# Batch 0 of a sparse attention with a dense layer behind it: halo keys on their own partitions, block keys scored apart, value rows cast in place, and two q turns moved into the output stage

## The chip, the cores and the metric

The kernel runs on one core of a Trainium2 chip. The metric is the device time of one execution in microseconds (us), over several executions (a run counts as slow when it is over 1.5% above the fastest of its kernel). A profile is one execution recorded by the hardware. In its lines PE is TensorE's matmuls, PEld its weight loads, DVE is VectorE, ACT is ScalarE, POOL is GpSimd, SP is SyncE.

## The reference, cut to what matters

```
q, k, v: (4 batches, 8 heads, 768 rows, 64) float32
k_sum = k in blocks of 32 rows: max over the block      # 24 block keys
v_sum = v in blocks of 32 rows: mean over the block     # 24 block values
scores_l = scale * q k^T, kept only where |row - col| < 16
scores_s = scale * q k_sum^T + log(32)
a = softmax over both together
x = a [v ; v_sum]                                       # (3072, 512) over all heads
h = x w_in (512 x 2048);  out = (h * sigmoid(1.702 h)) w_out (2048 x 512)
```

So each row looks at its neighbours within 15 rows and at 24 block rows.

## The kernel before

The work goes in eight halves: u = 0 to 7 are the two halves of batches 0 to 3. Each half has a dense input stage (`ph`, 64 matmuls of 384 columns), an activation, and a dense output stage (`po`, 48 of 512). The attention of half u+1 is slipped between the `po` matmuls of half u. Batch 0's first half has nothing before it: that is the prologue.

Tokens go in tiles of 64. In `kx` each tile has 128 key columns: 64 own keys, 24 block keys and 32 halo keys (neighbours; 8 columns stay empty), so one matmul scores all of them. The values `vw` need the rows in the same order on the partitions, so neighbours' rows have to cross partitions. DMAs inside SBUF do that:

```python
def before_even(w5, j0, j1):
    sp.dma_start(out=w5[96:112, j0:j1, 0], in_=w5[112:128, j0 - 1:j1 - 1, 1])
...                                   # after_even, before_odd, after_odd alike
def q_now(p):                         # first half of batch 0: two heads on 128 partitions
    return qz[p].rearrange("p t h c -> p (t h c)")[:, 0:HALF]
def s_turn(p):                        # scores of batch 0's first half, 64-row tiles
    big = st["S", p] = psb.tile([128, 1024], F32, name="ps_s", tag="big")
    for i in range(TH):
        for h in range(2):
            r = slice(h * 64, h * 64 + 64)
            pe.matmul(out=big[:, h * 512 + i * QT:h * 512 + i * QT + QT],
                      lhsT=kx[p][0][r, i, :], rhs=q_now(p)[r, i * QT:i * QT + QT],
                      start=True, stop=True)
```

Every other half keeps q padded with zeros (`qz`, both heads side by side), so that one matmul of 128 columns scores two heads. `psb`, tag "big", has two PSUM buffers that rotate between k turns, q turns, scores and values. The joint of the prologue, and the preparation of a batch in the second half of the one before:

```python
load_q(0, 0, 1) ... load_q(0, 3, 1)     # late q: second half of batch 0
s_exp(2); s_turn(3); v_zero(pool); s_exp(3)
v_cast(4, 0, act); v_cast(5, 0, act, 1); v_cast(5, 0, pool, 0)
load_w_in(0); load_w_in(1); load_w_in(2); load_w_in(3)
...
todo = {1: [lambda: tk(0, s)], 2: [lambda: tk(1, s)], 4: [lambda: tk(2, s)],
        6: [lambda: tk(3, s)], 8: [lambda: vsum(s, (0, 1, 2))],
        9: [lambda: vsum(s, (3, 4, 5)), lambda: vrows(s)],
        10: [lambda: tq(0)], 11: [lambda: tq(1)],
        13: [lambda: tq(2)], 14: [lambda: tq(3)]}
for nt in range(NT):                    # 16 groups of four ph matmuls
    ff_in(u, nt)
    for f in todo.get(nt, ()):
        f()
```

The softmax here doesn't subtract the row's maximum and nothing guards it: scores larger than these inputs give would overflow.

## Time and profile before

| | before |
|---|---|
| median of 3 runs (lowest to highest) | 241.51 us (241.22 to 242.05) |
| span of the profiled run | 239.8 us |
| first `ph` matmul (end of the prologue) | 26.63 us |
| input, output stage of half 0 | 13.96, 13.89 us |
| input, output stage of half 1 (prepares batch 1) | 16.16, 14.32 us |
| input, output stage of halves 3 and 5 (batches 2, 3) | 14.5, 13.89 us each |
| the same without a batch to prepare (halves 2, 4, 6) | 10.52, 13.9 us |

The stages are read on TensorE's timeline, from the first `ph` (or `po`) to the first of the next stage. The prediction below shows the busy row, the waits, TensorE's timeline and the chain.

VectorE's timeline in the prologue (start, duration, engine, line, operation, output and inputs, their shapes):

```profile
14.95 0.54 DVE L27 CAST qz<-ps_q 128x384 bf16<-128x384 f32 x1
15.42 0.41 DVE L27 CAST vw<-vf 64x512 bf16<-64x512 f32 x1
15.75 0.54 DVE L27 TENSOR_TENSOR a_sb<-a_sb,mk 128x768 bf16<-128x768 bf16 x1
18.84 1.53 DVE L27 TENSOR_TENSOR a_sb<-a_sb,mk 128x768 bf16<-128x768 bf16 x2 [2.55 <-ACT a_sb L27]
```

SyncE's share is not the halo copies, though: 22.9 of its 25.0 us lie between 41.3 and 65.2, where it issues batch 1's loads, the last of which TensorE then waits for (the q wait). On SyncE's timeline:

```profile
41.96 8.77 SPq L27 DMA_DIRECT2D kf<-in_k_dram  x8
...
57.69 8.09 SPq L27 DMA_DIRECT2D qf<-in_q_dram  x8
```

VectorE stands idle for 2.55 us in the middle of the prologue. Its casts take 0.41 and its mask multiplies 0.54.

### The profile page before, as it was taken

To read this page: it belongs to the slowest core of one execution; us is meant where nothing else is said; L and a number is where in the kernel's file an instruction comes from. 1 tells how busy PE (TensorE), PEld (TensorE's weight loads), DVE (VectorE), ACT (ScalarE), POOL (GpSimd) and SP (SyncE) were. 2 spreads that over 40 slices of the span, in tenths; PEclk is the share of its full clock that TensorE was granted. 3 is DMA by queue.
4 is the path that set the end of the run, shared out by engine and by line. 5 is a ranking of instruction groups with operands and counts; after the bars stand their busy time and mean duration, and the time that the engine had idled before them with its cause. 6 is when DMAs were issued, how large, how long until landed. Compare 5 with 4: busy or idle time off the path is not lost.

```text
span 239.8 us, 4567 instructions
## 1 busy us (share of the span) xinstructions
PE 226.7 (95%) x1743; PEld 132.7 (55%) x1743; DVE 128.5 (54%) x328; ACT 132.6 (55%) x225; POOL 69.9 (29%) x142
## 2 busy tenths in 40 slices
PE   7786979999989999999999999999999999999993
PEld 2533646556555555556665556556665565556541
DVE  5774945586964810486975800596957700770000
ACT  3856446455446467754565477545574478457510
POOL 6579960048640005773000013971000000000000
PEclk9999999999999999999999999999999999999999
DMA  6996999999993169995051199993051110111012
GB/s 194 286 192 103 238 231 206 222 218 218 202 260 98 45 156 219 201 220 173 0 113 46 44 195 202 231 223 119 14 102 45 44 46 0 44 46 44 0 44 89
DMA packets 76534, 32.21 MB, mean 134 GB/s; under 512 B 63856, under 2 KB 73440, under 8 KB 76512
## 3 DMA queue, kind: packets, MB, share of 16 engines
q1 hardware_dynamic: 72288, 27.73, 53.4%
q0 software_dynamic: 4224, 4.19, 10.7%
q8 instruction: 13, 0.21, 0.4%
q14 instruction: 9, 0.07, 0.1%
HBM read 27.26 MB, written 6.29 MB: 140 GB/s over the span
## 4 chain that ended last, share of the span: by engine, by line
PE 71%; SPq 10%; DMA 10%; DVE 3%; POOL 2%; issue 1%; ACT 0%; POOLq 0%; ACTq 0%
PE po L27 30%; PE ph L27 28%; SPq L27 10%; DMA w_in_sb<-in_moe_w_in_dram 7%; PE ps_av L27 4%; PE ps_s L27 3%; PE ps_t L27 2%; PE ps_x L27 2%; DMA kf<-in_k_dram 2%; DVE ks L27 1%; DMA qf<-in_q_dram 1%; PE ps_vs L27 1%; DVE kx L27 1%; POOL w_in_sb L27 1%; POOL vw L27 1%
## 5 line engine op out<-in xcount | busy, mean ns | idle before, releaser
L27 PE MATMUL po<-w_out_sb,gT 128*128 128x512 bf16 x384 | 95.6, 379 | 0.0
L27 PE MATMUL ph<-xT,w_in_sb 128*128 128x384 bf16 x512 | 91.6, 326 | 1.7 <-DMA w_in_sb<-in_moe_w_in_dram 1.6
L27 ACT ACTIVATE gT<-ph 128x384 bf16<-128x384 f32 x128 | 62.9, 491 | 40.2 <-PE ph L27 40.2
L27 PEld LDWEIGHTS <-w_in_sb 128*128 128x128 bf16 x512 | 48.7, 98 | 32.4 <-DMA w_in_sb<-in_moe_w_in_dram 2.4
L27 PEld LDWEIGHTS <-gT 128*128 128x128 bf16 x384 | 34.6, 98 | 28.0
L27 DVE TENSOR_TENSOR a_sb<-a_sb,mk 128x768 bf16<-128x768 bf16 x32 | 19.3, 609 | 55.8 <-ACT a_sb L27 55.0
L27 ACT ACTIVATE a_sb<-ps_s 128x768 bf16<-128x768 f32 x32 | 25.2, 809 | 23.0 <-PE ps_s L27 22.9
L27 POOL CAST kb<-kf 128x768 bf16<-128x768 f32 (+1 forms) x15 | 11.5, 765 | 78.8 <-DMA kf<-in_k_dram 78.8
L27 DVE TENSOR_TENSOR x_sb<-ps_av,rc 64x384 bf16<-64x384 f32 (+1 forms) x60 | 33.2, 554 | 1.4
L27 ACT ACTIVATE osb<-po 128x512 f32<-128x512 f32 x24 | 14.2, 593 | 31.3 <-issue 15.6
L27 POOL CAST vw<-vf 128x512 bf16<-128x512 f32 (+2 forms) x45 | 27.8, 659 | 3.2 <-DMA vf<-in_v_dram 3.0
L27 ACT ACT_TABLE_LOAD x16 | 20.5, 1283 | 1.1 <-PEq L792 0.8
L27 PEld LDWEIGHTS <-a_sb 128*128 128x128 bf16 (+1 forms) x264 | 13.8, 102 | 10.2 <-issue 2.7
L27 PE MATMUL ps_av<-vw,a_sb 128*128 128x130 bf16 (+1 forms) x216 | 15.8, 214 | 2.0 <-DMA vw<-vw 1.8
L27 PEld LDWEIGHTS <-kx 128*128 128x128 bf16 (+1 forms) x216 | 12.4, 97 | 6.6 <-issue 0.8
L27 PE MATMUL ps_s<-qz,kx 128*128 128x128 bf16 (+1 forms) x216 | 15.3, 213 | 0.1
L27 DVE COPY qz<-ps_t 64x768 bf16<-64x768 bf16 x24 | 13.3, 555 | 2.9 <-PE ps_t L27 2.5
L27 POOL CAST qb<-qf 128x768 bf16<-128x768 f32 (+1 forms) x14 | 11.4, 812 | 8.8 <-DMA qf<-in_q_dram 8.5
L27 DVE COPY xT<-ps_x 128x384 bf16<-128x384 bf16 x30 | 10.7, 358 | 3.7 <-PE ps_x L27 2.9
L27 PEld LDWEIGHTS <-x_sb 128*128 128x128 bf16 x96 | 7.7, 97 | 8.0 <-issue 1.8
L27 DVE RECIPROCAL rc<-ps_av 128x12 f32<-128x12 f32 (+1 forms) x32 | 7.2, 226 | 8.5 <-PE ps_av L27 8.2
L27 DVE TENSOR_REDUCE ks<-ps_t 128x24 bf16<-128x768 bf16 x12 | 11.4, 946 | 0.0
(61 smaller groups left out, 141.5 us busy)
## 6 DMA issues: line engine op xcount, KB each, us to landing
kf<-in_k_dram SPq DMA_DIRECT2D x32, 192.0 KB, 3.6
qf<-in_q_dram SPq DMA_DIRECT2D x32, 192.0 KB, 4.6
vf<-in_v_dram SPq DMA_DIRECT2D x24, 256.0 KB, 5.2
out_dram<-osb SPq DMA_DIRECT2D x24, 256.0 KB, 2.3
w_in_sb<-in_moe_w_in_dram POOLq DMA_DIRECT2D x4, 512.0 KB, 11.1
w_out_sb<-in_moe_w_out_dram POOLq DMA_DIRECT2D x4, 512.0 KB, 18.8
vw<-vs SPq DMA_DIRECT2D x6, 148.5 KB
vw<-vw SPq DMA_DIRECT2D x6, 99.0 KB, 2.9
```

Source lines behind the costliest of these rows:

```text
L27: r = f(*a, **kw)
```

## The change

In batch 0, `kx` keeps the 64 own keys and a 32-row neighbour strip on each side, each on the partitions that those rows have anyway; the block keys are scored by a matmul of their own. The value rows can then be cast from the staged float32 straight to where they belong, without a DMA. Both halves of batch 0 use this form. The intent is to take the copies through SyncE out of the prologue, and the weights forward.

```diff
+    def k_blocks(p, eng):
+        eng.tensor_copy(out=ksz[0:64, p, 0:nb], in_=st["m", p][0:64])
+        eng.tensor_copy(out=ksz[64:128, p, 32:32 + nb], in_=st["m", p][64:128])
+    def b_turn(p, half=0):                      # block scores, apart
...
+        r = slice(p % 2 * 64, p % 2 * 64 + 64)
+        pe.matmul(out=st["Bs", p // 2][r, 0:HALF], lhsT=ksz[:, p, :], rhs=q_now(p, half),
+                  start=True, stop=True)
+    def v_side(j, par, eng):                    # neighbours' value rows, in place
+        r, c = (slice(0, 32), j + 1) if par else (slice(96, 128), j - 1)
+        copy(eng, vw[0][r, 2 * j + par, :, 0:D], raw["v", c // 2][r, :, c % 2, :])
... the prologue's order
-    before_even(w50, 1, JH)                     # and ten more halo copies by DMA
-    load_q(0, 0, 1)                             # to load_q(0, 3, 1)
+    v_side(2, 1, dve)
     s_exp(2)
...
     s_exp(3)
+    v_cast(4, 0, dve)
...
     load_w_in(0)
+    v_sum(3)
+    v_idle(1)
+    v_cast(5, 0, dve, 0)
+    av_near(0)
...
     load_w_in(1)
+    s_mask(3, pool)
...
+    sp.dma_start(out=hold, in_=xT[0][0:16, 0:16])
+    for p in range(NP):
+        load_q(0, p, 1)
     load_w_in(2)
     load_w_in(3)
... preparation of the next batch
-                    10: [lambda: tq(0)], 11: [lambda: tq(1)],
-                    13: [lambda: tq(2)], 14: [lambda: tq(3)]}
+                    12: [lambda: tq(0)], 14: [lambda: tq(1)]}
+            later = {1: lambda: tq(2), 3: lambda: tq(3)}      # between the po groups
...
+            if u == 1 and nt == 7:
+                for p in range(NP):
+                    clear_qz(dve, p, 0)
+                    clear_qz(dve, p, 1)
```

The small DMA into `hold` reads `xT`, so that SyncE's queue stands until `xT` is there; the late q is issued behind it. One more thing changes: of the filler matmuls in the prologue (`warmth`, `v_idle`: their results are not used, they only keep TensorE busy), 17 behind the first eight become 5.

## The prediction

> **What bounds the kernel now.** I read the busy share of every engine first, then TensorE's waits, then the chain that ended last over the first 45 us, then TensorE's timeline around the places where it waits.
>
> ```profile
> PE 226.7 (95%) x1743; PEld 132.7 (55%) x1743; DVE 128.5 (54%) x328; ACT 132.6 (55%) x225; POOL 69.9 (29%) x142
> ```
>
> TensorE (PE) is busy for 226.7 of 239.8 us, and no other engine passes 55%. So time can only be won in TensorE's own work, or where it stands idle. The view of its waits says how little idle there is:
>
> ```profile
> PE ps_av L27 <- DMA vw<-vw: 1.8, 1, 1.8
> PE ph L27 <- DMA w_in_sb<-in_moe_w_in_dram: 1.6, 1, 1.6
> PE ps_t L27 <- POOL qb L27: 1.1, 1, 1.1
> ```
>
> One wait each: for the halo rows of the values, which a DMA copies from partition to partition inside SBUF; for the first weights; and, at 65.7 us, for batch 1's q. Everything else is the order of work. The kernel is a prologue (attention of batch 0, first half, until 26.6 us) and then eight pairs of a dense input stage (`ph`) and output stage (`po`), the latter with the next half's attention slipped between. The timeline of TensorE shows the joint:
>
> ```profile
> 20.67 0.38 PE L27 MATMUL ps_vt<-vw,E 128*128 128x512 bf16 x1
> ...
> 23.00 0.51 PE L27 MATMUL ps_av<-vw,a_sb 128*64 128x65 bf16 x21 [1.77 <-DMA vw<-vw]
> ...
> 26.63 5.65 PE L27 MATMUL ph<-xT,w_in_sb 128*128 128x384 bf16 x32
> 33.83 0.82 PE L27 MATMUL ph<-xT,w_in_sb 128*128 128x384 bf16 x4 [1.56 <-DMA w_in_sb<-in_moe_w_in_dram]
> ```
>
> The first 32 `ph` matmuls are half of the stage (two of four weight chunks); then the third chunk is not there. The chain confirms that what ends last here is not attention but the weights, behind GpSimd's (POOL) queue:
>
> ```profile
> 17.37 1.71 POOL vw L27 x2
> 19.07 2.28 POOL w_in_sb L27 x3
> 21.36 15.92 DMA w_in_sb<-in_moe_w_in_dram
> 37.28 0.05 issue
> 37.33 0.82 PE ph L27 x4
> ```
>
> The fourth chunk is issued at 21.4 and lands at 37.28, and TensorE starts on it 0.05 us later: the whole input stage stands on this transfer. Its packet records say why it takes so long: a chunk of 512 KB takes 2.54 us when alone (the w_out chunks end at 38.30, 40.84, 43.38) but 4.0 us while the late q loads and the halo copies run too (w_in chunks end at 24.36, 28.37, 32.37).
>
> After 40.6 us it is nearly solid. Measured on the timeline, the output stage of half 0 takes 13.89 (40.59 to 54.48); batch 1's preparation stage 16.16 (54.48 to 70.64), against 14.5 for the same stage of batch 2 (109.50 to 124.00): the 1.7 us are the wait for q (1.07) and VectorE (DVE), which is busy without a gap from 56.4 to 66.6.
>
> **What the Trainium skill says.** "DMA: Bandwidth & Descriptors", Anatomy of one DMA, gives a fixed cost of about 2 us, mostly the receipt after the last byte. The trace agrees in size: the last packet of the third chunk ends at 32.37 and TensorE goes on at 33.83, 1.46 us later. The same page, Issuing engines are not separate DMA queues, says that DMAs of all issuers share the same 16 engines and interleave: that is the 2.54 against 4.0 us per chunk. "ScalarE: Activation LUTs", What ACT_TABLE_LOAD costs, has 1283 ns per load plus a drain; the trace has 1283 ns as the mean of 16 loads. It matters below, because it stands ahead of the first exp of each output stage. No page tells how the two rotating PSUM buffers below are handed on; that is read from the kernel.
>
> **The change, part by part.**
>
> *1. Prologue: the wait and GpSimd's detour go.* Value rows and their neighbours are now cast from the staged tile straight to their partitions, so the 1.77 us wait for the copies goes. I chained the new order of instructions with durations of the old profile. The values arrive as before: by the packet records the six transfers end 1.25 apart, the fourth at 14.52 (it landed 1.3 later, at 15.83), the fifth at 15.79, and the sixth, into which the halo copies came, at 17.57. Without them I put it at 17.05 and its landing at 18.3 (the old run cast it from 18.69). VectorE: the last k_max ends at about 13.1 (four reductions of 0.94, the side copies 0.27 to 0.33), then casts and masks at 0.41 to 0.54 bring it to 17.7. ScalarE (ACT): fourth exp until 16.9, block exp 17.3, then the last values from 18.3 to 18.7. So the last v_sum pair runs at about 18.7 to 19.1 instead of 20.45 to 20.9: 1.7 us earlier. From there to the first `ph` the old order took 26.63 - 20.45 = 6.2, of which 1.8 is the wait; the new one has the same chain (four small copies, four normalisations of 0.54 on VectorE, transposes, xT copies) of some 4.2. Start about 22.9: 3.7 earlier.
>
> *2. Weights.* GpSimd reaches the first w_in issue after its casts at about 15.8 (k and q casts until 11.4; side copies 1.0; the casts 0.64 to 0.72 each, with one wait for k_max at 13.1), where it was 19.03. The packets started 1.6 after the issue (20.61), so 17.4 now. The halo copies (0.4 MB) are gone and the late q loads start only after xT. Alone, five chunks (four w_in and the first w_out) take 12.7; the old run took 38.30 - 20.61 = 17.7, a penalty of 5.0 for 1.2 MB of strangers; two thirds of those remain, penalty 3.3. The first w_out chunk then ends at 33.4 and lands at 34.9. The w_in chunks land in time, so the stage takes 64 x 0.163 + 4 q turns x 0.29, with 0.3 at the start: 11.9 instead of 13.96. 22.9 + 11.9 = 34.8, and w_out allows 34.9: the first output stage starts at 34.9 instead of 40.59, **5.7 earlier**.
>
> *3. Output stage of half 0 grows.* Half 1 of batch 0 now also scores apart. Per pair of heads: scores 0.28 (12 small matmuls, prologue's pitch) against 0.34; block scores 384 columns, 0.16, new; near values 0.34 against 0.34; block values 3 x 130 columns, 0.17, new. That is +0.27, times four **+1.1**. ScalarE gets two more exps of 0.49, VectorE fewer instructions; neither is last there. Net at 54.48: -4.6.
>
> *4. Batch 1's preparation.* Turning q2 and q3 in the output stage takes the q wait (1.07) off. But qz of batch 0 is no longer zero-padded, so 16 memsets of 0.218 (3.5 us) now stand on VectorE between the fourth k and the block sums, in the stretch where it has no gap. With T the start of the stage, VectorE's k work ends T+10.4 as before, memsets T+14, block sums T+14.6, q0 copies T+15.8. TensorE is through at T+14.6 (14.5, as batch 2, plus 0.9 for VectorE's late buffers, less 0.7 for two turns moved), runs one `po` group (0.87) and meets the first scores at T+15.5: they wait 0.3 to 0.8 for q0. Then the rest of part 5. In all about **-0.4** against the old 30.5 for both stages.
>
> *5. Two q turns between the scores, batches 2 and 3.* They are taken out of the input stage (0.34 each) and put in the output stage, so work is the same. But turned q and scores share two rotating PSUM buffers: the order becomes s0, q2, s1, and s1 must wait for s0's exp, where s0 and s1 used to have a buffer each. In batch 2's stage (start F = 124.00) the exp ends at F+2.76 behind the table load; s1 would start at F+2.06+0.34 = F+2.4. Wait 0.4. Later VectorE's q copies (1.14 a pair) delay the first normalisation, and v1, which reuses v0's buffer, loses about 0.2. So **+0.6** each for batches 2 and 3, 1.2 together; batch 2 and 3 had no q wait to win back.
>
> Sum: -5.7 + 1.1 - 0.4 + 1.2 = -3.8. 241.5 - 3.8 = 237.7 us, 1.6% faster.
>
> **Rivals.** (a) *Everything early stays won, nothing is paid later*: if the buffers rotate more kindly than I read them and the memsets hide, -5.7 + 1.1 - 1.5 = -6.1, 235.4. For it: the two-buffer wait is read from code, no old view shows it. Against: VectorE has no gap at 56 to 66. (b) *The transfer is the bound anyway*: the gain of the prologue is lost to w_out or batch 1's loads. These began landing in the old run when w_out ended (47.6) and run at about 0.22 MB/us for 21 us; if GpSimd reaches w_in only at 18, all moves with it: about 240. For it: the old chain runs through this very transfer; against: the gap in DMA traffic at 18 to 20 us (share 0.16), which the earlier issue fills. (c) *VectorE becomes the bound of the prologue*: it takes over side copies and casts; if they run slower beside GpSimd (a 128x384 cast took 0.36 alone and up to 0.77 in company), the start slips by 1 to 1.5: 239.
>
> **Range and chances.** The prologue is chained by hand through five engines, +-1; the later costs +-0.8; GpSimd's issue +-0.8. Together about 1.7 either way. 2% is 236.7, one microsecond below my figure: faster by more 0.28, within 2% 0.68, slower 0.04.
>
> **What would show it.** Right: no wait for vw<-vw in the prologue; first `ph` at 22 to 23.3; first w_in issue near 15.8; no or a short wait for w_out at the first `po`, near 34.9; output stage of half 0 at 15.0; no wait for qb in batch 1, but one for qz at its first scores; batches 2 and 3 taking 0.6 longer from their preparation to the end of the output stage. Wrong: a first `ph` after 24.5, a w_in issue after 18, batch 2's stages unchanged in length, or the memsets hidden.

## More of the kernel before

The page's summary of the chain that ended last, by engine:

```profile
PE 71%; SPq 10%; DMA 10%; DVE 3%; POOL 2%; issue 1%; ACT 0%; POOLq 0%; ACTq 0%
```

## The result, and the profile after

| | before, same rounds | after |
|---|---|---|
| median (lowest to highest), 4 runs each | 241.78 us (241.22 to 242.21) | 248.2 us (248.09 to 250.15) |
| span of the profiled run | 239.8 us | 246.6 us |

The ratio is 1.0286 (95% interval 1.023 to 1.0342): the changed kernel is slower. All ratios here are the mean time of one kernel's fast runs over that of the other's of the same rounds, so not quite the ratio of the medians quoted. The predicted 237.7 us, its range, and its likeliest class (within 2%) are all missed.

The stages say where the time came from:

| stage | before | after | difference | predicted |
|---|---|---|---|---|
| prologue, to the first `ph` | 26.63 | 28.14 | +1.5 | -3.7 |
| half 0, input | 13.96 | 13.36 | -0.6 | -2.1 |
| half 0, output | 13.89 | 15.83 | +1.9 | +1.1 |
| half 1, both (prepares batch 1) | 30.48 | 32.60 | +2.1 | -0.4 |
| halves 3 and 5, both | 28.4 each | 29.3 each | +0.9 each | +0.6 each |

That is 6.7 of the 6.8 us between the spans: half 2 gives 0.1 back, and the rest lies behind the start of the last stages.

Three rows of the page of the changed kernel: busy time of each engine, the granted TensorE clock in 40 slices (in tenths; 9 is full), and the chain by engine:

```profile
PE 228.5 (93%) x1727; PEld 132.4 (54%) x1751; DVE 130.4 (53%) x322; ACT 134.2 (54%) x228; POOL 76.6 (31%) x170
...
PEclk9998899999999999999999999999999999999998
...
PE 70%; DVE 15%; DMA 7%; ACT 3%; issue 2%; SPq 2%; ACTq 0%; DVEq 0%
```

SyncE's share of the chain has gone from 10% to 2%, and VectorE's has risen from 3% to 15%. Most of SyncE's fall is not the copies: batch 1's loads are no longer on the path, as its q is no longer what TensorE waits for, and VectorE's work for batch 1 has taken their place. That the copies are off the path shows in the waits below. The clock row shows an 8 in slices 4 and 5, which the profiled run of the kernel before does not have; other runs of that kernel have a mean granted clock down to 0.98, so a stretch at half clock is not a mark of the changed kernel alone. The waits of TensorE (total, times, longest):

```profile
PE ps_s L27 <- DVE qz L27: 3.3, 1, 3.3
PE ps_vs L27 <- DVE vw L27: 2.1, 3, 1.5
PE ps_av L27 <- DVE vw L27: 1.6, 1, 1.6
PE ps_q L27 <- DVE qz L27: 1.4, 1, 1.4
```

Waits for the halo copies and for w_in are gone. All four that replace them name VectorE. On TensorE's timeline they lie thus:

```profile
20.14 0.48 PE L27 MATMUL ps_av<-vw,a_sb 128*64 128x65 bf16 x19 [1.61 <-DVE vw L27]
...
22.37 0.38 PE L27 MATMUL ps_vs<-vw,E 128*128 128x512 bf16 x1 [1.52 <-DVE vw L27]
...
38.90 0.49 PE L27 MATMUL ps_q<-ident,qb 128*128 128x128 bf16 x3 [1.37 <-DVE qz L27]
...
75.78 0.51 PE L27 MATMUL ps_s<-qz,kx 128*128 128x128 bf16 x6 [3.31 <-DVE qz L27]
```

The first two are in the prologue, the third in the input stage of half 0, the fourth in the output stage of half 1. What VectorE and GpSimd did before the first two:

```profile
17.70 2.38 DVE L27 CAST vw<-vf 32x512 bf16<-32x512 f32 x1
...
18.20 1.64 POOL L27 DMA_DIRECT2D w_in_sb<-in_moe_w_in_dram  x2
...
19.85 2.19 POOL L27 TENSOR_TENSOR a_sb<-a_sb,mk 128x768 bf16<-128x768 bf16 x1
20.01 0.53 DVE L27 TENSOR_TENSOR a_sb<-a_sb,mk 128x768 bf16<-128x768 bf16 x1
20.48 2.05 DVE L27 CAST vw<-vf 128x512 bf16<-128x512 f32 x2
```

A cast of 32 x 512 takes 2.38 us here; a larger one took 0.41 before. The row with two casts, 2.05 together, is 1.84 and 0.28 one by one. VectorE is not busy in these 4 us so much as held. The slow cast of 1.84 us lies beside GpSimd's mask multiply, which runs from 19.85 to 22.04, and ends 0.28 after it. The cast of 2.38 us lies mostly beside two issues of weight loads, in front of that multiply.

The third and fourth wait, on the timeline of SyncE's queue and of VectorE (that of the latter from two stretches):

```profile
28.07 2.38 SPq L27 DMA_DIRECT2D qf<-in_q_dram  x4
...
38.02 0.36 DVE L27 CAST qb<-qf 128x384 bf16<-128x384 f32 x1 [3.37 <-DMA qf<-in_q_dram]
...
69.31 4.66 DVE L27 MEMSET qz<- 64x192 uint32 x16
```

The late q is issued at 28.07 and its last part can be cast at 38.02. All four casts stand in VectorE's order ahead of the first copy of turned q (`qz`), so TensorE waits for it. In batch 1, sixteen memsets stand in front of the block sums and of the q copies.

### The profile page after: what moved, and what is told of

Read it like the earlier page. It is cut to its first block, busy times and chain, and to the rows that moved or that the text cites. A ratio compares the mean times of both kernels' runs of the same rounds, so it can differ in the third digit from the quotient of the medians.

```text
span 246.6 us, 4562 instructions
## 1 busy us (share of the span) xinstructions
PE 228.5 (93%) x1727; PEld 132.4 (54%) x1751; DVE 130.4 (53%) x322; ACT 134.2 (54%) x228; POOL 76.6 (31%) x170
## 4 chain that ended last, share of the span: by engine, by line
PE 70%; DVE 15%; DMA 7%; ACT 3%; issue 2%; SPq 2%; ACTq 0%; DVEq 0%
PE po L27 27%; PE ph L27 26%; PE ps_av L27 5%; DVE qz L27 4%; PE ps_s L27 3%; DMA qf<-in_q_dram 3%; DVE x_sb L27 3%; DVE kx L27 3%; PE ps_t L27 2%; PE ps_x L27 2%; DMA vf<-in_v_dram 2%; DMA kf<-in_k_dram 2%; DVE vw L27 2%; ACT a_sb L27 2%; SPq L27 2%
## 5 line engine op out<-in xcount | busy, mean ns | idle before, releaser
L27 PE MATMUL po<-w_out_sb,gT 128*128 128x512 bf16 x361 | 92.1, 379 | 1.1
L27 PE MATMUL ph<-xT,w_in_sb 128*128 128x384 bf16 x512 | 90.2, 326 | 0.0
L27 PEld LDWEIGHTS <-w_in_sb 128*128 128x128 bf16 x512 | 49.2, 98 | 30.9 <-issue 1.5
L27 DVE TENSOR_TENSOR x_sb<-ps_av,rc 64x384 bf16<-64x384 f32 (+1 forms) x56 | 30.9, 555 | 1.6 <-PE ps_av L27 0.2
L27 POOL CAST vw<-vf 128x512 bf16<-128x512 f32 (+2 forms) x49 | 31.2, 674 | 1.2 <-DMA vf<-in_v_dram 0.6
L27 ACT ACT_TABLE_LOAD x16 | 20.5, 1283 | 1.1 <-PEq L858 0.8
L27 PE MATMUL ps_s<-qz,kx 128*128 128x128 bf16 (+1 forms) x240 | 14.8, 208 | 4.0 <-DVE qz L27 3.3
L27 PEld LDWEIGHTS <-a_sb 128*128 128x128 bf16 (+1 forms) x240 | 12.4, 106 | 10.6 <-issue 3.9
L27 PEld LDWEIGHTS <-kx 128*128 128x128 bf16 (+1 forms) x240 | 11.3, 97 | 11.5 <-DVE qz L27 5.3
L27 POOL CAST qb<-qf 128x768 bf16<-128x768 f32 (+1 forms) x16 | 12.4, 772 | 8.0 <-DMA qf<-in_q_dram 7.2
L27 PE MATMUL ps_x<-ident,x_sb 128*128 128x128 bf16 x96 | 10.6, 219 | 0.8 <-DVE xT L27 0.6
```

Source lines behind the costliest of these rows:

```text
L27: r = f(*a, **kw)
```

## The experiments

My theory after reading the traces was that five things make the loss: VectorE's casts held in the prologue, TensorE's half clock behind that, the late q, the memsets in batch 1, and the late turns. The expectations call "port lock" the theory that VectorE's casts and GpSimd cannot use SBUF at the same time. The main rivals were that the weight issues hold the casts and not the multiply, and that the transfers bound the first input stage whatever the prologue does. Twelve kernels ran; all gave correct results. Each is compared with the kernel before in the same rounds; "the changed kernel" is the one of the section above.

### The mask multiply from GpSimd to VectorE

```diff
-    s_mask(3, pool)
+    s_mask(3, dve)
```

> The changed kernel with the fourth mask multiply back on VectorE. Theory (port lock): a VectorE copy from SBUF cannot run while GpSimd holds the port they share, whether GpSimd multiplies, casts or issues a weight load. Then the four weight issues now follow one another (0.8 us each, about 18.2 to 21.4) and hold the side cast of the values until 21.4 instead of 20.08, while the cast held by the multiply until 22.04 comes free: little is won, 0 to 0.7 us, 247.5 to 248.2. Rival (only the multiply blocks, the issues do not): the side cast takes 0.4, both PE waits of 1.6 and 1.5 shrink, and 2 to 3 us are won, about 245.5.

Measured: median 248.76 us (247.46 to 250.26), ratio 1.0267 (1.0203 to 1.033). VectorE and GpSimd in the prologue of this kernel, from their timelines:

```profile
17.89 0.82 DVE L27 CAST vw<-vf 32x512 bf16<-32x512 f32 x1
18.64 0.54 DVE L27 TENSOR_TENSOR a_sb<-a_sb,mk 128x768 bf16<-128x768 bf16 x1
19.11 1.03 DVE L27 CAST vw<-vf 128x512 bf16<-128x512 f32 x2
...
18.39 3.11 POOL L27 DMA_DIRECT2D w_in_sb<-in_moe_w_in_dram  x4
```

The same cast takes 0.82 instead of 2.38, and the next two 0.41 and 0.69 instead of 1.84 and 0.28, although GpSimd is issuing weight loads nearly all the while (for the first 0.5 us it still casts). So the issues alone do not hold a cast for 2 us: that reading falls, and the multiply is what does. An issue may still cost some 0.4, as the last and smallest cast is slower here. The first `ph` comes at 24.16 instead of 28.14. Yet no time was won: the input stage now takes 17.9 us instead of 13.36, because its q turns wait 2.7 us for `qb` and 2.6 us for `qz`, and the output stage starts 0.6 later than in the changed kernel. There are two bounds behind one another. Half 1 lost another 1.1 us (33.71), with the clock at half from 76.4 to 79.8.

### The late value casts from VectorE to ScalarE

```diff
-    v_side(2, 1, dve)          # and v_cast(4, 0, dve), v_cast(5, 0, dve, 0)
     v_cast(3, 0, act)
+    v_side(2, 1, act)
...
-    v_cast(5, 0, act, 1)
+    v_cast(4, 0, act)
+    v_cast(5, 0, act)
```

> The changed kernel with the three value casts that VectorE did late in the prologue (a side cast of 32 partitions, 128x512, 128x256) on ScalarE; the fourth mask stays on GpSimd. Theory (port lock): ScalarE is not held by GpSimd, so the casts take 0.6 each, the near products start at about 18.3 instead of 20.14, no wait for vw remains, and the first ph comes at about 24.5 to 25 instead of 28.14: about 245. Rival (VectorE and ScalarE just have too much work in the prologue, the 2.38 us were queueing): ScalarE becomes late instead, first ph after 27, within 1 us of 248.2.

Measured: 249.3 us (247.31 to 251.2, one run slow), ratio 1.0275 (1.0226 to 1.0324). First `ph` at 24.45, input stage 17.59. The multiply stayed on GpSimd and took 1.66 us instead of 2.19; the difference is as long as the one mask multiply on VectorE that lay beside it in the changed kernel (0.53). So leaving the multiply and moving the casts heals the prologue as well; it looks as if the two engines disturb each other, and the stage behind it gives everything back again (the output stage starts at 42.04, not 41.50).

### Both together

The two edits above in one kernel.

> Both edits: fourth mask on VectorE, the three casts on ScalarE. Theory (port lock): no VectorE copy from SBUF is left next to the weight issues; first ph at 23.5 to 24.5, clock stays at full speed, total about 4 us less: 244. The masks (two SBUF inputs) may still be held a little. Rival (prologue is bound by the arrival of the values or of the weights): first ph no earlier than 26, and a wait for w_in appears.

Measured: 249.75 us (247.39 to 250.5), ratio 1.0305 (1.0247 to 1.0363). First `ph` at 23.98, output stage at 40.67 instead of 41.50. In the profiled run the late q was issued at 23.72, 4.35 us earlier than in the changed kernel. VectorE's timeline, and then TensorE's:

```profile
37.19 0.36 DVE L27 CAST qb<-qf 128x384 bf16<-128x384 f32 x1 [1.78 <-DMA qf<-in_q_dram]
...
38.07 0.49 PE L27 MATMUL ps_q<-ident,qb 128*128 128x128 bf16 x3 [2.71 <-DVE qz L27]
```

The last part is cast only 0.83 us earlier than in the changed kernel. The late q shares the DMA engines with 2 MB of w_in and with w_out, and lands at about 37 to 38 whether it is issued at 23.7 or at 28.1. That is why 4.2 us of prologue are worth 0.8 us at the output stage. These 0.8 us were lost in turn: the output stage of half 1 took 21.34 us instead of 18.49, with the granted clock at half from 74.1 to 80.9.

### More filler matmuls in the two gaps

```diff
-    v_idle(1)                  # ahead of the near values
+    v_idle(8)
...
     v_recip(0)
+    v_idle(6)
```

> The changed kernel with 13 more filler matmuls in the two places where TensorE idled for 1.6 and 1.5 us. The trace granted half the clock from 23.1 to 26.5 us. Theory (the clock fell because of the two gaps, and cost time): the clock stays at 1.0 and the first ph comes 0.7 to 1.2 us earlier, about 247.2. Rival (the halved clock hid behind VectorE's chain): clock 1.0, first ph within 0.3 of 28.14, 248. If the clock falls all the same, the gaps were not its cause.

Measured: 247.81 us (245.5 to 249.1), ratio 1.0231 (1.0161 to 1.03); at 2% that is unclear, and its interval overlaps that of the changed kernel. The windows view says what the filler did. Its columns are busy time with instructions for PE, PEld, DVE, ACT and POOL, then granted clock, DMA share and GB/s. First the changed kernel, in two windows of 3.4 us:

```profile
19.70:23.10 3.40, 1.45 (x29) 0.98 (x29) 3.00 (x6) 0.00 (x0) 3.39 (x4) 1.00 1.02 155
23.10:26.50 3.40, 3.40 (x44) 2.01 (x43) 1.60 (x6) 2.03 (x4) 3.21 (x6) 0.50 1.24 205
```

Then the kernel with filler:

```profile
19.70:23.10 3.40, 2.86 (x35) 1.50 (x35) 2.90 (x6) 0.00 (x0) 3.39 (x4) 1.00 1.04 160
23.10:26.50 3.40, 3.13 (x54) 2.03 (x52) 2.67 (x8) 2.87 (x6) 3.21 (x6) 1.00 1.24 206
```

Where TensorE was busy for 1.45 of 3.40 us, the next 3.4 us ran at half clock; with 2.86 of 3.40 they did not. In the profiled run the first `ph` came at 26.87 instead of 28.14 with the casts held just as long (2.38): the half clock is worth 1.3 us there, by one execution of each kernel. In the other three runs of this kernel the mean clock was 0.99 again (where it fell is not recorded), so filler is not a sure cure.

### The memsets of qz out of batch 1's preparation

```diff
-            if u == 1 and nt == 7:
-                for p in range(NP):
-                    clear_qz(dve, p, 0)
-                    clear_qz(dve, p, 1)
...
                 else:
                     tx(p)                    # batch 0's second half
+                    clear_qz(dve, p, 1)
...
         if u == 0:
+            for p in range(NP):
+                clear_qz(dve, p, 0)
```

> The changed kernel with the 16 memsets of qz taken out of batch 1's preparation: half 0 is cleared on VectorE during the first input stage, where it is idle, half 1 behind the xT copies of the first output stage. Theory: the memsets (4.66 us in the trace) are what makes the first scores of batch 1 wait 3.3 us; the wait falls to 0 to 0.5 and the total by about 3: 245.2. Rival (VectorE's k work, which ends at 69.3, or the arrival of q sets that stage): the wait stays above 2, total within 1 us of 248.2.

Measured: 245.59 us (244.87 to 247.73), ratio 1.0166 (1.0112 to 1.0221). Half 1 takes 13.85 + 15.43 = 29.28 us instead of 32.60, and the wait of the first scores for `qz` is gone. What is left at the scores, on TensorE's timeline:

```profile
75.00 0.49 PE L27 MATMUL ps_s<-qz,kx 128*128 128x128 bf16 x6 [0.30 <-ACT a_sb L27]
```

This is the wait for a PSUM buffer behind the exp, which the prediction's part 5 spoke of. The memsets are worth 3.3 us of the stage, the largest part that any single edit gave back. The input stage of half 0 took 14.70 in this profiled run (13.36 in the changed kernel), so not all of it shows in the time.

### The two late turns back in the input stage

```diff
-                    12: [lambda: tq(0)], 14: [lambda: tq(1)]}
-            later = {1: lambda: tq(2), 3: lambda: tq(3)}
+                    10: [lambda: tq(0)], 11: [lambda: tq(1)],
+                    13: [lambda: tq(2)], 14: [lambda: tq(3)]}
```

> The changed kernel with the four q turns of each batch back in the input stage. Theory (the late turns take one of two PSUM buffers between the scores, so scores wait for the exp before): the output stages of batches 2 and 3 go from 15.4 to 13.9 and their input stages from 13.8 to 14.5, 0.9 less for each; batch 1 stays as it is, since the memsets hold q's copies wherever they stand: about 246.5. Rival (the turns are free, the longer output stage has another cause): no change, 248.2.

Measured: 249.34 us (249.19 to 253.29, one run slow), ratio 1.0304 (1.0263 to 1.0344). Batches 2 and 3 are back at 14.50 + 13.89, 0.87 us less each. But half 1 takes 34.54 us instead of 32.60, as a q turn now waits 4.3 us for the `qz` copies behind the memsets, and more windows were at half clock (20.4 to 27.2, 40.8 to 44.2, 78.4 to 81.8). The edit could not be judged by its time while the memsets stood where they did.

### The late q casts spread between the turns

```diff
-                cast_q(dve, p, 1)
+                todo[7 + 2 * p] = [lambda p=p: cast_q(dve, p, 1)]
                 todo[8 + 2 * p] = [lambda p=p: (q_turn(p, 1), q_copy(p, dve, 1))]
```

> The changed kernel with the four casts of the late q halves put one by one between the q copies, instead of all ahead of them. Theory: VectorE, in order, held the copy of q0 behind the cast of q3, whose data landed at 37.94; with the casts spread the wait of 1.37 in the first input stage goes, total about 1.3 less: 246.9. Rival (the late arrival of q3 itself binds, it is issued only at 28.07): the wait moves to the fourth turn and stays above 0.7.

Measured: 248.52 us (247.69 to 250.66), ratio 1.0286 (1.0229 to 1.0343). The input stage takes 11.83 us and its `qz` wait is gone. But in this execution the first `ph` came at 29.37, after two half-clock windows (20.5 to 27.3), and half 1 took 33.63 us, with another such window (75.1 to 78.5). The wait is cured; the time does not show it.

### The late turns alone, in the kernel before

> The kernel before with one part of the change alone: two of four q turns of each batch moved to the output stage. Theory (two buffers): batches 2 and 3 lose 0.9 each as in the changed kernel; batch 1 wins its q wait of 1.07 and pays the buffers: net +0.7 to +1.8, 242.5 to 243.6. Rival (the loss in the changed kernel came from elsewhere): the before's time less the q wait, 240.7.

The edit is that of the change, 12 and 14 with `later`, and nothing else. Measured: 243.76 us (243.15 to 244.16), ratio 1.0074 (1.0044 to 1.0104). Batches 2 and 3 take 13.83 + 15.43, again 0.87 us more each than before; half 1 takes 30.59 against 30.48. So the late turns cost 1.7 us on their own and win nothing in batch 1 of that kernel. Measured in these stages and in time they agree; the profiled run also started its first output stage 0.65 later, ahead of anything that the edit touches.

### All of it together, with late q issued early

The edits of the two moves in the prologue, the memsets and the spread casts; late turns only in batch 1; and the late q right behind the values instead of behind `xT`:

```diff
     load_v(0)
+    for p in range(NP):
+        load_q(0, p, 1)
...
-    sp.dma_start(out=hold, in_=xT[0][0:16, 0:16])
-    for p in range(NP):
-        load_q(0, p, 1)
```

> All mends together: fourth mask on VectorE, three casts on ScalarE, qz cleared outside batch 1's preparation, q casts spread, the late q loads issued straight after the values (as the transfers stand idle at 17 to 20 us) instead of behind xT, and two q turns in the output stage for batch 1 only. Theory: first ph at 24, first input stage 11.9 (no wait for q), output stage of half 0 still 15.8, batch 1's two stages 29.3 as in e_clear, batches 2 and 3 back at 28.4: the sum puts the span at 236 and the time at 237.8, 1.6 per cent under the kernel before. Rival (the weights now bind: the q loads delay them): waits for w_in of 1 to 2 us, 239 to 240.

Measured in five rounds: 238.69 us (238.04 to 241.09) against 241.47 before, ratio 0.9892 (0.9853 to 0.9931). First `ph` at 24.46, input stage 11.72, half 1 14.1 + 15.44, batches 2 and 3 14.5 + 13.89, and no window at half clock before the end.

### The same, with late q behind xT

```diff
     load_v(0)
-    for p in range(NP):
-        load_q(0, p, 1)
...
+    sp.dma_start(out=hold, in_=xT[0][0:16, 0:16])
+    for p in range(NP):
+        load_q(0, p, 1)
```

> The same with the late q loads issued behind xT, as in the changed kernel. Theory (what the earlier prologue wins is lost to the arrival of the late q, which shares the transfers with weights already queued and takes some 12 us): first ph at 24, input stage 15 to 16 instead of 11.9, total 3 to 4 us above e_best: 241 to 242. Rival (only the order of casts on VectorE made those waits): input stage under 12.5, same time as e_best.

Measured in the same rounds: 240.87 us (240.39 to 241.29), ratio 0.9963 (0.9941 to 0.9985). First `ph` at 24.22, input stage 14.84 instead of 11.72. This separates the last term: where q is issued is worth 3.1 us of the stage and 2.2 us of the time, with everything else healed.

### The block scores at full width

```diff
-    ksz = keep.tile([128, NP, 64], BF16, name="ksz")
+    ksz = keep.tile([128, NP, 128], BF16, name="ksz")   # odd p in columns 64 to 127
...
-        pe.matmul(out=st["Bs", p // 2][r, 0:HALF], ..., start=True, stop=True)
+        pe.matmul(out=st["Bs", p // 2][:, 0:HALF], ..., start=(p % 2 == 0), stop=(p % 2 == 1))
```

This is the combined kernel with one edit more: two block-score matmuls of 128 columns of weights add into one tile, where two of 64 wrote one half each.

> e_best with the block scores of two pairs of heads as two accumulating matmuls of all 128 columns (the other pair's columns zero) instead of one of 64 columns each. In the changed kernel a block-score matmul of 384 columns, with what it holds up, took 0.28 where 384 columns at full width take 0.163, and the first po after it took longer. Theory (changing the width of the array between matmuls costs time): output stage of half 0 goes from 15.8 to about 15.3, total 0.3 to 0.5 less than e_best. Rival (the width is free, the 0.28 are the weight load of 12 small matmuls before): no change.

Measured in the same rounds: 238.01 us (237.28 to 238.68), ratio 0.9847 (0.9823 to 0.9872). The output stage of half 0 is 15.59 instead of 15.83. This is the best version found, 1.5% faster than the kernel before (within 2%, but the interval excludes 1). That it beats the version with 64 columns in time is not shown: the two intervals overlap. Two rows of its page:

```profile
PE 227.1 (96%) x1751; PEld 131.9 (56%) x1751; DVE 129.0 (54%) x320; ACT 134.9 (57%) x230; POOL 74.3 (31%) x169
...
PE 84%; DMA 7%; DVE 3%; POOL 2%; issue 2%; ACT 1%; SPq 1%; POOLq 0%; ACTq 0%
```

TensorE now carries 84% of the chain, where it had 71% before and 70% after the change; neither SyncE nor VectorE is left in it to speak of.

### The multiply ahead of the weight issues

```diff
+    s_mask(3, pool)
     load_w_in(0)
...
-    s_mask(3, pool)
```

> The changed kernel with GpSimd's mask multiply put ahead of its first two weight issues instead of behind them. In the traces so far the side cast of the values on VectorE takes 2.38 us when the multiply stands behind two issues (it ends 0.23 after the multiply's recorded start) and 0.82 when there is no multiply; the issues alone do not hold it. Theory A (the cast is held only until the multiply gets going): with the multiply first the cast ends 0.2 to 0.3 after the multiply's start, near 18.5, and takes under 1 us; the next VectorE cast from SBUF is held until the multiply's end instead. Theory B (GpSimd's multiply owns the port from the moment it is queued to its end): the cast ends 0.2 to 0.3 after the multiply's end, near 20.2, again over 2 us. In both the weights are issued some 2 us later, so no gain in time is expected: 248 to 250.

Measured: 250.74 us (250.26 to 252.0), ratio 1.0366 (1.0339 to 1.0394); the weights are issued from 20.03, and the input stage takes 18.63 us, with 4.2 us of waits for the late q and the clock at half from 40.2 to 43.6, but none for weights. VectorE's timeline, then GpSimd's:

```profile
17.93 2.43 DVE L27 CAST vw<-vf 32x512 bf16<-32x512 f32 x1
20.28 0.54 DVE L27 TENSOR_TENSOR a_sb<-a_sb,mk 128x768 bf16<-128x768 bf16 x1
...
18.45 1.62 POOL L27 TENSOR_TENSOR a_sb<-a_sb,mk 128x768 bf16<-128x768 bf16 x1
```

With the multiply in front, the cast is held until 20.36, 0.28 us after the multiply's end (20.08). The casts behind it, beside the weight issues, take 0.43 and 0.72. So the hold is tied to the multiply and lasts to its end. In the changed kernel two issues stood ahead of the multiply, and there the cast ended 0.23 us after the multiply's recorded start. Why it was already held while the issues ran, when issues alone do not hold it, stays open: no run told it.

## Why the prediction was wrong

**Part 1 failed in its durations.** It put the first `ph` at 22.9; it came at 28.14. Three terms make the 5.2 us. VectorE's list was longer than counted: the last k_max ended at 14.04, not at 13.1, and with both moves healed the first `ph` still came at 23.98; that is 1.1. The casts were given the old profile's 0.41 although GpSimd had been given a mask multiply to run beside them. From the side cast at 17.70 on, a mask multiply and the last two casts take VectorE to 22.45, where its next instruction starts; with the mask multiply off GpSimd the same instructions went from 17.89 to 20.06. That is 2.6. And TensorE, which had stood for 1.61 and 1.52 us, got half the clock from 23.1 to 26.5 in the profiled run; with filler in both gaps it did not, and the first `ph` came some 1.3 earlier. Together these are 5.0 of 5.2. What taking out the fillers might do, the prediction did not count.

The Trainium skill states the second term, on a page that the prediction did not draw on. "SBUF — State Buffer", Who interferes with whom, says that VectorE and GpSimd share one pair of SBUF ports under an exclusive lock, that casts can take it, that a two-input VectorE multiply contends for its read side, and that the other engine "fully blocks (not throttle)". The runs agree in kind: 2.43 us beside the multiply, 0.82 without. The page also says that ScalarE never waits there. The kernel with the casts on ScalarE agrees as far as it goes: beside GpSimd's casts and weight issues they took 0.61 to 0.63 each, as ScalarE's casts of this size do in all the traces. But they were through at 19.83 and the multiply began at 20.24, so no run shows ScalarE beside the multiply. The third term is in "TensorE: Matmul & The Clock Gate", The HAM clock gate, which gives windows of 3413 ns after which an idle TensorE runs at half its clock. The trace has the half clock, 0.50 for one window of 3.4 us, though TensorE was not idle in all of the window before (last section).

Rival (c), VectorE as the bound of the prologue, was right in kind. It even quoted a cast at 0.36 alone and 0.77 in company, but sized the slip at 1 to 1.5 us.

**Part 2 followed the wrong transfer.** The first w_in issue came at 18.20, not 15.8: GpSimd waited for k_max until 14.10, and four casts took 3.29 together. Even so TensorE never waited for weights in the changed kernel. The step that failed is the sentence that the late q loads start only after `xT`. It was used only for what it spares the weights. The late q itself was not chained on: issued at 28.07, cast at 38.02, with a wait of 1.37 in the input stage; the kernel before had issued it at 19.99. The rest of the stage (13.36 - 1.37 = 12.0) is the predicted 11.9. This bound would have held had part 1 been right: the healed prologue won 4.2 us and lost all but 0.8 in this stage. Rival (b) had the transfer as the bound, but of w_out or batch 1's loads, not of q.

**Part 3 was right in kind and too small.** The stage took 15.83, not 15.0. On TensorE's timeline:

```profile
43.02 1.04 PE L27 MATMUL po<-w_out_sb,gT 128*128 128x512 bf16 x4
43.99 0.35 PE L27 MATMUL ps_s<-qz,kx 64*128 64x64 bf16 x12
44.27 0.35 PE L27 MATMUL ps_b<-qz,ksz 128*64 128x384 bf16 x1
44.55 1.90 PE L27 MATMUL po<-w_out_sb,gT 128*128 128x512 bf16 x8
```

From start to start (43.99 - 43.02 = 0.97 for the first line), near and block values take 0.50 a pair, as predicted (0.34 + 0.17). Two things were missing. Block scores, put at 0.16, take 0.28 in three of four places. And a group of four `po` matmuls takes 0.96 instead of 0.86 where a matmul on a part of the array comes next; in the combined kernel ("All of it together"), whose stage is as long and whose trace has every record of it, seven of the twelve groups stand so, 0.7 us together. "TensorEngine Tiling (Array Packing)", Key Properties, says that a change of tiling mode drains TensorE, which fits: at full width the block scores take 0.17 in the same three places, and the stage lost 0.24, while the `po` group behind them, with narrow scores next, still takes 0.96. The figures are shown; that a drain makes them is only argued.

**Part 4 had the mechanism and missed the size.** It expected a wait of 0.3 to 0.8 for q0; it was 3.31. The sixteen memsets took 4.66, not 3.5 (0.29 each, not 0.218). VectorE's k work ended 12.0 us into the stage, not 10.4: the short copies inside `kx`, which took 0.36 to 0.60 for three before, took 1.00 to 1.31. GpSimd was at casts or memsets beside each of them. In the kernel with the memsets moved, the fourth three took 0.36 with GpSimd idle, and the others 0.79 to 1.24 beside its work; but in the kernel before, three beside its casts took only 0.38 to 0.60. So company is part of it, and the rest stays open. The q wait did go, as predicted. Instead of -0.4, half 1 lost 2.1; without the memsets it took 29.28, which is 1.2 less than before.

**Part 5 was right in mechanism, and the size came out larger.** Each of batches 2 and 3 lost 0.87 instead of 0.6. The late turns alone in the kernel before gave the same 0.87. The wait of s1 for s0's exp, put at 0.4, is there in batch 2:

```profile
131.03 0.49 PE L27 MATMUL ps_s<-qz,kx 128*128 128x128 bf16 x6 [0.30 <-ACT a_sb L27]
```

So the sum went wrong most in its largest term: -5.7 was predicted up to the first output stage; 41.50 against 40.59 is +0.9. Half 1 was next (+2.1 for -0.4). Two of the prediction's four signs of being wrong came true: the first `ph` after 24.5 and a w_in issue after 18. Its range was also narrow by its own figures: +-1, +-0.8 and +-0.8 add up to 2.6, or 1.5 if they are independent, not 1.7; neither covers a miss of 10 us. The part of the change that the intent was about works: in the best version that stage starts at 36.66 (3.9 earlier), after taking away what the change had put in the way.

## What to carry to other kernels

Durations from an old profile hold only as long as each instruction keeps its company: when work is moved so that VectorE and GpSimd both use SBUF at once, look at every cast that will lie beside it. Chain each moved transfer forward to its first use, also one that is moved only to make room for another. When an edit heals a wait and the time stays, look for the next bound at the end of that same stage before giving the edit up: here two single edits won 4 us in the prologue and nothing in time, and paid in full only when the late q came earlier too.

## What the Trainium skill lacked or had wrong

- "SBUF — State Buffer", Who interferes with whom: the lock explains the casts that were held until 0.28 us after GpSimd's multiply ended (2.43 and 1.84 us). It does not explain the cast held for 2.38 us of which 1.65 lay beside two weight issues with the multiply queued behind them and not yet begun by its record; beside issues alone the casts took 0.41 to 0.72.
- "TensorE: Matmul & The Clock Gate", HAM oscillation: it puts the limit at idle gaps of over about 3.4 us. Here two gaps of 1.61 and 1.52 us with work between them were enough: TensorE was busy for 1.45 of 3.40 us, and the next window ran at half clock. With 2.86 of 3.40 it did not. TensorE's busy time alone is not the rule either: counted on in steps of 3.41 us, the changed kernel's window from 70.91 held 1.51 us and full clock followed, while the window from 17.06 in the kernel with the spread casts held 1.88 and half clock followed. The page's next section says that short idles can do it too, without a size; no run here shows what measure the clock goes by.
- "TensorEngine Tiling (Array Packing)", Key Properties: it names the drain at a change of mode without a size. Here block scores of 64 columns of weights took 0.28 us in the flow, and 0.17 with 128 columns, for the same 384 columns of data; and four `po` matmuls took 0.96 ahead of a matmul on a part of the array, 0.86 ahead of others.
